# Splitting z and v in the opening of an attention and mixture-of-experts kernel

## Chip, cores and metric

The kernel runs on one core of a Trainium2 chip, as one program. The metric is the device time of one execution in microseconds. The core's engines are TensorE (PE; its weight loads are PEld), VectorE (DVE), ScalarE (ACT), GpSimd (POOL) and SyncE (SP), which issues most DMAs. Each works through its own queue in order.

## The reference

```python
def _attn_ref(u, v, z):                 # u, v: 8 x 3072 x 256, z: 8 x 3072 x 64
    scores = (1.0 / S) * np.matmul(z, z.transpose(0, 2, 1))
    attn = np.maximum(scores, 0.0) ** 2
    return (u * np.matmul(attn, v)).astype(np.float32)

def _moe_ref(x, w_gate, w1, w2, capacity):      # 8 experts, 1024 hidden, capacity 768
    expert_idx = np.argmax(x @ w_gate, axis=1)  # gate_w: its softmax probability
    # the first `capacity` tokens of each expert, in order, are kept
    h = np.maximum(np.einsum('ecd,edf->ecf', disp, w1), 0.0)
    y = np.einsum('ecf,efd->ecd', h, w2)
    # out[i] = gate_w[i] * y[expert, slot] for kept tokens, else 0
```

The inputs are float32, and so is the output of 24576 x 256.

## The kernel before

The experts fill up with the early tokens, so attention is computed only for the first 14 blocks of 512 queries (two batches and two blocks more), with a fallback for other data. Products run in float16 with each float32 operand split in two: a high half, and a low half that is the residue. Three matmuls (high by high, high by low, low by high) make one product.

For a block of queries the keys are taken in pairs of 128-row tiles. For each pair `team` (line 935) computes the scores: six matmuls of 64 rows and 512 columns (line 958), two at a time in the upper and lower 64 partitions. For that `zz` holds z transposed twice: in plane 0 the high half lies in partitions 0 to 63 and the low half above it, in plane 1 the two are swapped. `follow` (line 964) then makes the pair's weights: relu of each key tile and the square on ScalarE (lines 975 and 980), the high half as a cast on VectorE (`hi`, line 984) and the residue on VectorE (`lo`, line 993). The sums (line 1141) are matmuls of 128 x 256 with these weights and v's two halves: 24 for a pair, into four accumulators (`c`), two key tiles (`jj`) each. v's halves come from `v_piece`: high on ScalarE (line 524), low on VectorE (line 527).

z's groups of four tiles come from `z_group` (line 409): `hi` scales and rounds, `lo` (lines 421 and 422) copies the high half behind the place of the low half, so that three 64-wide parts stand in a row (high, low, high), and takes the residue. `tr` turns columns 0 to 127 and columns 64 to 191 of each tile on TensorE, four transposes for each plane (line 433), and `ev` copies each plane out of PSUM (line 437). Groups 3 to 5 go another way (`z_wide`, with DMA transposes).

All scaling is by powers of two from a maximum. v's scale needs all of the first batch's v: absolute sums and maxima of each piece (lines 493 and 75), a maximum over them (line 501), GpSimd's all-reduce (line 79), and two steps on the exponent bits (lines 60 and 62).

The order of the opening is written out by hand. `to_scores` and `to_sums` call `go(chain, n)`, which issues the next n steps of a chain; `A` are v's maxima, `G` z's groups, `V` v's pieces (tiles 0, 1, and 2 with 3), `follow[0]` and `follow[1]` the weights of pairs 0 and 1, `third` those of pair 2, `Z` the z groups that are turned by DMA. `warm_up(n)` issues n matmuls whose results are not used; they fill TensorE's time. After `to_sums`, a planner (`weave`, line 268) issues each chain's next step as soon as its modelled engine clocks (`clk`, with the costs written beside each step) let it fit. `steps` (line 1054) gives the order of the sums: in the first block all four accumulators of a pair, and in each accumulator both key tiles, one after the other.

Of the kernel before, what the change touches and what calls it, by code (L numbers as in the profile page):

```python
# [9 lines left out]
F32 = mybir.dt.float32  # L10
F16 = mybir.dt.float16
I32 = mybir.dt.int32
AF = mybir.ActivationFunctionType
ALU = mybir.AluOpType
# [4 lines left out]
P = 128  # L19
# [9 lines left out]
def attention_moe_kernel(ctx: ExitStack, tc: tile.TileContext, u, v, z, w_gate, w1, w2, out, cap):  # L29
# [311 lines left out]
    def prepare(bt, first=False, swap=(), held=None):  # L341
# [67 lines left out]
        def z_group(g):  # L409
            sl = slice(4 * g, 4 * g + 4)  # L410
            st = Bag()

            def hi():
                st.zhl = sb.tile([P, 4, 3 * DQ], F16, tag="zhl", name="zhl", bufs=3)
                if g < 2:
                    ts(st.zhl[:, :, 0:DQ], bt.zraw[:, sl], bt.zs, ALU.mult)
                else:
                    nc.scalar.activation(st.zhl[:, :, 0:DQ], bt.zraw[:, sl], AF.Copy, scale=bt.zs)

            def lo():  # L420
                nc.vector.tensor_copy(st.zhl[:, :, 2 * DQ:3 * DQ], st.zhl[:, :, 0:DQ])
                nc.vector.scalar_tensor_tensor(out=st.zhl[:, :, DQ:2 * DQ], in0=bt.zraw[:, sl], scalar=bt.zs,
                                               in1=st.zhl[:, :, 0:DQ], op0=ALU.mult, op1=ALU.subtract)

            def tr():
                if g < 2:
                    st.tp = [ps.tile([P, 4, P], F16, tag="sc", name="ztp", bufs=6) for r in range(2)]
                else:
                    t = ps.tile([P, 2, 4, P], F16, tag="sc", name="ztp", bufs=6)
                    st.tp = [t[:, r] for r in range(2)]  # L430
                for r in range(2):
                    for k in range(4):
                        nc.tensor.transpose(st.tp[r][:, k, :], st.zhl[:, k, r * DQ:r * DQ + P], ident)

            def ev(r):
                def f():
                    (nc.scalar.copy if r and g != 1 else nc.vector.tensor_copy)(
                        bt.zz[:, r, g * BLK:(g + 1) * BLK].rearrange("p (t q k) -> p t k q", t=2, k=2),
                        st.tp[r].rearrange("p (t k) q -> p t k q", k=2))
                return f  # L440

            return [[("ACT", 0.4, hi, None) if g > 1 else ("DVE", 0.3, hi, None)], [("DVE", 0.6, lo, key("zl", g))],
                    [("PE", 0.45, tr, None)],
                    [("DVE" if g == 1 else "ACT", 0.6 if g == 1 else 0.48, ev(1), key("ze", g)),
                     ("DVE", 0.6, ev(0), key("z", g))]]
# [74 lines left out]
        def v_piece(t0, k):  # L520
            o, i, a = slice(t0, t0 + k), t0 // 4, t0 % 4

            def hi():
                nc.scalar.activation(bt.v2[:, o, 0, :], bt.vraw[i][:, a:a + k], AF.Copy, scale=bt.vs)

            def lo():
                nc.vector.scalar_tensor_tensor(out=bt.v2[:, o, 1, :], in0=bt.vraw[i][:, a:a + k], scalar=bt.vs,  # L527
                                               in1=bt.v2[:, o, 0, :], op0=ALU.mult, op1=ALU.subtract)
                for j in range(t0 + 2, t0 + k, 2):
                    done[key("v", j // 2)] = clk["DVE"]  # L530

            return [[("ACT", 0.19 + 0.21 * k, hi, None)], [("DVE", 0.06 + 0.285 * k, lo, key("v", t0 // 2) if t0 + k > t0 // 2 * 2 + 1 else None)]]

        def factor():
# [68 lines left out]
        def go(c, n=1):  # L603
            for _ in range(n):
                assert c.item() is not None
                c.emit()
# [20 lines left out]

        def to_sums(follow, more):

            go(A[2])  # L630
            go(follow[0], 3)
            go(A[3])
            go(follow[0])
            go(A[4])
            warm_up(2)
            third = more()[0]
            go(G[2])
            go(A[6])
            go(A[5])
            go(follow[1], 2)  # L640
            vr = Chain([[("DVE", 0.2, v_red, None)], [("POOL", 0.4, v_all, None)], [("DVE", 0.6, v_bits, key("vs"))]], -2,
                       need_max("m", NM))
            go(vr, 3)
            go(follow[0])
            warm_up(11)
            go(G[2])
            warm_up(2)
            more()
            warm_up(3)
            Z = Chain(pipe([z_wide(t0) for t0 in range(NT, JT, ZW)]) + [[z_swap(0), z_swap(1)]], -2, late)  # L650
            for t, k in ((0, 1), (1, 1), (2, 2)):
                V[t] = Chain(v_piece(t, k), -2, done[key("vs")])
            go(V[0])
            go(V[1])
            go(V[0])
            go(V[1])
            go(follow[1])
            go(V[2])
            go(G[2])
            go(follow[1], 2)  # L660
            go(V[2])
            go(G[2])
            go(Z)
            go(third, 2)
            go(Z, 4)
            go(third)
            for i in range(2, JT // 2):
                Chain(v_piece(2 * i, 2), -2, done[key("vs")], gate=("pair", i - 2 + (2 < i < 6)))
# [194 lines left out]
    def attention(blocks, hook):  # L863
# [100 lines left out]
        def follow(p, s, w, t):  # L964
# [14 lines left out]
                sq[p] = sb.tile([P, 2, w], F32, tag="a", name="a")  # L979
                nc.scalar.activation(sq[p], sct.pop(p), AF.Square)  # L980

            def hi():
                hl = sb.tile([P, 2, nt, 2, HB], F16, tag="hl", name="hl", bufs=NHL)
                nc.vector.tensor_copy(hl[:, :, :, 0, :], sq[p].rearrange("p j (t k) -> p j t k", k=HB))  # L984
                prs[p] = lambda h, jj, c: hl[:, jj, c // 2, h, c % 2 * P:(c % 2 + 1) * P]
                if cornered(p):
                    own = prs[p]
                    prs[p] = lambda h, jj, c: corner[n][:, 2 * h + jj, c * P:(c + 1) * P] if c < 2 else own(h, jj, c - 2)
                sq[p] = (sq[p], hl)

            def lo():
                a, hl = sq[p]
                nc.vector.tensor_sub(hl[:, :, :, 1, :], a.rearrange("p j (t k) -> p j t k", k=HB), hl[:, :, :, 0, :])  # L993

            def turn(c):
                def f():
# [22 lines left out]
            def room_for():  # L1019
# [2 lines left out]
            st = [[("ACT", 0.05 + w * 0.00084, relu(0), None), ("ACT", 0.05 + w * 0.00084, relu(1), (aid, "r", k))],  # L1022
                  [("ACT", 0.09 + w * 0.00168, square, (aid, "s", k))],
                  [("DVE", 0.07 + w * 0.00107, hi, None, bt.key("vs"), room_for), ("DVE", 0.29 + w * 0.0021, lo, (aid, "a", p))]]
            if p + 1 < NP and cornered(p + 1):
                st.append([turn(0), turn(1)])
            if cc == CC and (ib, g // 2) in bt.kept:
# [26 lines left out]
        def steps():  # L1054

            for n, (_, _, _, cc) in enumerate(blocks):
                i = 0
                while i < NPAIR:
                    both = cc == CC and (i == 0 and not (opening and n == 0) or i == NPAIR - 2)
                    for h in range(2 if both else 1):  # L1060
                        for j in range(2 if both else 1):
                            for c in (2 * h, 2 * h + 1) if both else range(cc):
                                calm[0] = n * NPAIR + i < NP - 2 and both and (h + j > 0 if i else n > 0 and h + j < 2)
                                turning[0] = both and (i > 0 or n > 0 and h + j < 2)
                                yield n * NPAIR + i + j, c
                    i += 2 if both else 1

        def ld_u(n):
# [32 lines left out]
            scores_to(0)  # L1101
        clear[0] = open_bank
        operand = {}
        for p, c in steps():
            where[:] = p, c
            n, g = at(p)
            bt, ib, c0, cc = blocks[n]
            i = p % NPAIR
            if c == 0:
                hook(p)  # L1110
                done.setdefault(("pair", p), clk["PE"])
                loads_to(p + 4)
                if i == 0:
                    acc[n] = {}
                if i == NPAIR // 2:
                    ld_u(n)
            if c % (cc // 2) == 0:
                scores_to(p + 3 if p > 3 else p + 2 if p or c else 0)
                weave()
            if c == 0:  # L1120
                if is_next(p):
                    take(p)
                clk["PE"] = max(clk["PE"], need((aid, "a", p), bt.key("v", g),
                                                *([(aid, "d", n)] if cornered(p) else [])) + HOP)
                operand[p] = prs.pop(p)
            a = operand[p]
            if i == 0 and c % 2 == 0:

                k = bank[0] - 2
                if k in held:  # L1130
# [2 lines left out]
                bank[0] += 1  # L1133
                acc[n][c // 2] = ps.tile([P, 2, D], F32, tag="acc", name="acc", bufs=2)
            o = acc[n][c // 2][:, c % 2]
            for jj in (0, 1):
                j = 2 * g + jj


# [2 lines left out]
                                     stop=(i == NPAIR - 1 and jj + h == 2), skip_group_check=True)  # L1142
                op("PE", 0.328, 0.0)
                weave()
            if i == NPAIR - 1 and c % 2:
                drain(n, c // 2)
            if c == cc - 1:
                through.add(p)
                operand.pop(p)
            if i == NPAIR - 1 and c == cc - 1:  # L1150
# [359 lines left out]
```

## Time and profile before

| | |
|---|---|
| median of 3 runs | 777.61 us (776.28 to 780.22) |
| profiled execution, own time | 778.41 us |
| its span | 776.5 us |
| PE, DVE, ACT, POOL busy | 766.8, 514.4, 401.1, 116.6 us |
| granted TensorE clock | 0.998 of full speed |

The span is the time between the first and the last event of the trace; the execution's own time has a little around it. Busy time counts warm-up matmuls as well. In rows of the timeline, several like instructions in a row are merged (x2, x24), and what stands in brackets is the idle time of the engine before them and what ended it.

### The profile page before, as it was taken

The numbers are of one execution on the slowest core, as the hardware profiler recorded it, in microseconds if no ns is written. First come the engines' busy times: TensorE is split into PE (matmuls) and PEld (weight loads), VectorE is DVE, ScalarE is ACT, GpSimd is POOL, SyncE is SP. The second block draws the span as 40 slices with busy tenths as digits, with TensorE's granted clock in tenths as the row PEclk, the third lists the DMA queues.
The fourth block names the chain that finished last, engine by engine and source line by source line (L and its number), as shares of the span: only waits on it lengthen the run. The fifth ranks groups of instructions, "written<-read, shape, count | busy, mean of one in ns | idle before, by whom it ended". The sixth has DMA issues, their size and how long they took to land.

```text
span 776.5 us, 16291 instructions
## 1 busy us (share of the span) xinstructions
PE 766.8 (99%) x6474; PEld 572.3 (74%) x6474; DVE 514.4 (66%) x1134; ACT 401.1 (52%) x690; POOL 116.6 (15%) x122
## 2 busy tenths in 40 slices
PE   9999999999999999999999999999999999999996
PEld 3777878888887787878888877876666656666664
DVE  7998789754308799875554268889576575575741
ACT  6985558433016667573530057675455464463541
POOL 0000020210202020202022020203320321313302
PEclk9999999999999999999999999999999999999999
DMA  7699949999978979698789949882898955944001
GB/s 224 124 351 137 288 104 241 178 220 195 189 149 166 326 177 228 164 235 190 166 153 197 201 134 214 305 233 58 236 264 286 319 147 215 296 120 185 28 15 45
DMA packets 283831, 149.49 MB, mean 193 GB/s; under 512 B 229742, under 2 KB 255675, under 8 KB 283745
## 3 DMA queue, kind: packets, MB, share of 16 engines
q1 hardware_dynamic: 278848, 135.57, 71.8%
q0 software_dynamic: 4896, 12.79, 5.3%
q8 instruction: 52, 0.85, 0.4%
q14 instruction: 35, 0.28, 0.1%
HBM read 36.25 MB, written 59.92 MB: 124 GB/s over the span
## 4 chain that ended last, share of the span: by engine, by line
PE 88%; issue 3%; DMA 3%; DVE 2%; POOL 1%; SPq 1%; ACT 0%; POOLq 0%; ACTq 0%; DVEq 0%
PE acc L1141 51%; PE hps L1287 14%; PE yps L1311 14%; PE sc L958 8%; DMA ld<-kept 2%; DMA vraw<-in_v 1%; POOL out L86 1%; PE lg L722 1%; DVE hl L993 1%; SPq L375 0%; DVE hl L984 0%; DVE wm L75 0%; DVE xr L707 0%; DVE v L527 0%; SPq L369 0%
## 5 line engine op out<-in xcount | busy, mean ns | idle before, releaser
L1141 PE MATMUL acc<-v,hl 128*128 128x256 f16 x2280 | 260.7, 273 | 1.0 <-DVE v L527 0.6
L1141 PEld LDWEIGHTS <-hl 128*128 128x128 f16 x2280 | 219.5, 98 | 36.4 <-issue 9.2
L975 ACT ACTIVATE r<-sc 128x512 f32<-128x512 f32 (+1 forms) x212 | 105.5, 550 | 142.2 <-PE sc L958 140.0
L1311 PE MATMUL yps<-wt,hh 128*128 128x256 f16 (+1 forms) x776 | 126.8, 324 | 0.0
L1287 PE MATMUL hps<-fxt,wt 128*128 128x384 f16 (+2 forms) x816 | 126.7, 317 | 0.0
L993 DVE TENSOR_TENSOR hl<-a,hl 128x1024 f16<-128x1024 f32 (+1 forms) x106 | 118.1, 1114 | 3.5
L1287 PEld LDWEIGHTS <-wt 128*128 128x128 f16 x816 | 77.8, 98 | 47.1
L1311 PEld LDWEIGHTS <-hh 128*128 128x128 f16 x776 | 75.7, 98 | 48.4
L86 POOL DMA_INDIRECT disp<-xr,slot x54 | 56.8, 1051 | 359.7 <-issue 215.5
L1141 PE MATMUL acc<-v,ld 128*128 128x256 f16 x960 | 109.0, 273 | 0.6 <-DMA ld<-kept 0.6
L980 ACT ACTIVATE a<-r 128x1024 f32<-128x1024 f32 (+1 forms) x106 | 102.6, 968 | 5.0 <-DVE hl L993 2.6
L1141 PEld LDWEIGHTS <-ld 128*128 128x128 f16 x960 | 92.7, 98 | 13.9 <-issue 2.1
L984 DVE CAST hl<-a 128x1024 f16<-128x1024 f32 (+1 forms) x106 | 67.5, 637 | 45.8 <-ACT a L980 45.0
L1273 DVE SCALAR_TENSOR_TENSOR hh<-hps,hh 128x384 f16<-128x384 f32 (+2 forms) x136 | 70.6, 530 | 34.6 <-ACT hh L1272 33.1
L1272 ACT ACTIVATE hh<-hps 128x384 f16<-128x384 f32 (+2 forms) x136 | 63.4, 470 | 48.9 <-PE hps L1287 47.3
L86 POOL DMA_INDIRECT out<-ys,sid x48 | 53.3, 1111 | 129.9 <-DVE ys L1320 77.1
L958 PE MATMUL sc<-zz 64*128 64x512 f16 (+1 forms) x636 | 68.5, 355 | 0.0
L704 ACT ACTIVATE xr<-x,rsr 128x256 f16<-128x256 f32 x54 | 24.4, 500 | 82.9 <-DVE rsr L62 66.7
L1317 ACT ACTIVATE ys<-yps,sg 128x256 f32<-128x256 f32 x48 | 22.7, 474 | 76.9 <-PE yps L1311 70.4
L1320 DVE SCALAR_TENSOR_TENSOR ys<-yps,sg,ys 128x256 f32<-128x256 f32 x47 | 22.7, 483 | 53.0 <-ACT ys L1317 50.6
L1141 PE MATMUL acc<-v,nx 128*128 128x256 f16 x504 | 57.4, 273 | 0.0
L1141 PEld LDWEIGHTS <-nx 128*128 128x128 f16 x504 | 49.0, 98 | 6.5 <-issue 0.8
(135 smaller groups left out, 485.7 us busy)
## 6 DMA issues: line engine op xcount, KB each, us to landing
out<-zero SPq DMA_DIRECT2D x48, 512.0 KB
kept<-hl SPq DMA_DIRECT2D x40, 512.0 KB
wraw<-in_moe_w SPq DMA_DIRECT2D x32, 512.0 KB
vraw<-in_v SPq DMA_DIRECT2D x18, 512.0 KB
u<-in_u SPq DMA_DIRECT2D x13, 512.0 KB
zraw<-in_z SPq DMA_DIRECT2D x2, 768.0 KB
zz<-zz SPq DMA_DIRECT2D x4, 384.0 KB
xt<-xr SPq DMA_TRANSPOSE x54
```

The source lines that it names most:

```text
L86: r = nc.gpsimd.indirect_dma_start(out=dst, out_offset=bass.IndirectOffsetOnAxis(ap=idx, axis=0), in_=src, in_offset=None, bounds_check=bo ...
L704: return lambda: nc.scalar.activation(st.x16[:, c, 0:D], st.x[:, c, :], AF.Copy, scale=st.rs[:, c:c + 1])
L958: nc.tensor.matmul(s[jj][:, 0:w], lhsT=bt.zz[rows, (kl + jj) % 2, j * P:(j + 1) * P], rhs=bt.zz[rows, (ql + jj) % 2, q0:q0 + w], start=(i ...
L975: nc.scalar.activation(sct[p][:, jj, :], s[jj][:, 0:w], AF.Relu)
L980: nc.scalar.activation(sq[p], sct.pop(p), AF.Square)
L984: nc.vector.tensor_copy(hl[:, :, :, 0, :], sq[p].rearrange("p j (t k) -> p j t k", k=HB))
L993: nc.vector.tensor_sub(hl[:, :, :, 1, :], a.rearrange("p j (t k) -> p j t k", k=HB), hl[:, :, :, 0, :])
L1141: nc.tensor.matmul(o, lhsT=a(h, jj, c), rhs=bt.v2[:, j, l], start=(i + jj + h + l + c % 2 == 0), stop=(i == NPAIR - 1 and jj + h == 2), sk ...
L1272: Chain([[("ACT", 0.05 + w * 0.00083, lambda: nc.scalar.activation(th, src, AF.Relu), None)], [("DVE", 0.07 + w * 0.00104, lambda: nc.vect ...
L1273: [("DVE", 0.07 + w * 0.00104, lambda: nc.vector.scalar_tensor_tensor(out=tl, in0=src, scalar=0.0, in1=th, op0=ALU.max, op1=ALU.subtract), ...
L1287: nc.tensor.matmul(o, lhsT=wx.w1[:, d, wp, f * P:(f + 1) * P], rhs=sx.xt[:, xp * DC + d, a:a + w], start=(q == 0), stop=(q == len(seq) - 1))
L1311: nc.tensor.matmul(y[:, 0 if end else l], lhsT=hid(i, f)[:, sl], rhs=w[:, l], start=(f + i == 0 and l != 1), stop=(f == FC - 1 and i == 1) ...
```

## The change

`z_group` keeps only two parts (high, low). For plane 0 the tile is turned whole as before. For plane 1 the low and the high half are turned apart, each into its half of the partitions, so four transposes of 64 columns each way take the place of four of 128 columns, and `lo` no longer copies. The third group's `lo` runs on GpSimd as a product and a subtraction. In the opening, pair 0's residue and pair 1's square, high half and residue are made one key tile at a time, v's tiles 2 and 3 get their low halves one by one, and the sums of pairs 0 and 1 run over all four accumulators with the first key tile and then over all four with the second. The hand-written order is rearranged, and 16 warm-up matmuls stand where 18 stood in `to_sums`.

```diff
-                st.zhl = sb.tile([P, 4, 3 * DQ], F16, tag="zhl", name="zhl", bufs=3)
+                st.zhl = sb.tile([P, 4, 2 * DQ], F16, tag="zhl", name="zhl", bufs=3)
...
-                nc.vector.tensor_copy(st.zhl[:, :, 2 * DQ:3 * DQ], st.zhl[:, :, 0:DQ])
-                nc.vector.scalar_tensor_tensor(out=st.zhl[:, :, DQ:2 * DQ], in0=bt.zraw[:, sl], scalar=bt.zs,
-                                               in1=st.zhl[:, :, 0:DQ], op0=ALU.mult, op1=ALU.subtract)
+                if g < 2:
+                    nc.vector.scalar_tensor_tensor(out=st.zhl[:, :, DQ:], in0=bt.zraw[:, sl], scalar=bt.zs,
+                                                   in1=st.zhl[:, :, 0:DQ], op0=ALU.mult, op1=ALU.subtract)
+                else:
+                    t = sb.tile([P, 4, DQ], F32, tag="u", name="zsc", bufs=1)
+                    nc.gpsimd.tensor_scalar(out=t, in0=bt.zraw[:, sl], scalar1=bt.zs, scalar2=None, op0=ALU.mult)
+                    nc.gpsimd.tensor_tensor(out=st.zhl[:, :, DQ:], in0=t, in1=st.zhl[:, :, 0:DQ], op=ALU.subtract)
 
...
-                for r in range(2):
-                    for k in range(4):
-                        nc.tensor.transpose(st.tp[r][:, k, :], st.zhl[:, k, r * DQ:r * DQ + P], ident)
+                for k in range(4):
+                    nc.tensor.transpose(st.tp[0][:, k, :], st.zhl[:, k, :], ident)
+                for k in range(4):
+                    for r in (1, 0):
+                        nc.tensor.transpose(st.tp[1][DQ * (1 - r):DQ * (2 - r), k, :], st.zhl[:, k, DQ * r:DQ * (r + 1)],
+                                            ident)
...
-            return [[("ACT", 0.4, hi, None) if g > 1 else ("DVE", 0.3, hi, None)], [("DVE", 0.6, lo, key("zl", g))],
+            return [[("ACT", 0.4, hi, None) if g > 1 else ("DVE", 0.3, hi, None)], [("DVE", 0.6, lo, key("zl", g)) if g < 2 else ("POOL", 1.0, lo, key("zl", g))],
...
+            def lo_one(j):
+                def f():
+                    nc.vector.scalar_tensor_tensor(out=bt.v2[:, t0 + j, 1, :], in0=bt.vraw[i][:, a + j], scalar=bt.vs,
+                                                   in1=bt.v2[:, t0 + j, 0, :], op0=ALU.mult, op1=ALU.subtract)
+                return f
+
...
+            if first and t0 == 2:
+                return [[("ACT", 0.61, hi, None)], [("DVE", 0.38, lo_one(0), None), ("DVE", 0.38, lo_one(1), key("v", 1))]]
...
+            go(G[2])
             go(A[2])
             go(follow[0], 3)
             go(A[3])
...
             warm_up(2)
             third = more()[0]
+            warm_up(3)
             go(G[2])
+            go(follow[0])
+            go(follow[1])
             go(A[6])
             go(A[5])
-            go(follow[1], 2)
-            vr = Chain([[("DVE", 0.2, v_red, None)], [("POOL", 0.4, v_all, None)], [("DVE", 0.6, v_bits, key("vs"))]], -2,
+            vr = Chain([[("DVE", 0.2, v_red, None)], [("POOL", 0.4, v_all, None)], [("DVE", 0.4, v_bits, key("vs"))]], -2,
                        need_max("m", NM))
             go(vr, 3)
             go(follow[0])
-            warm_up(11)
-            go(G[2])
+            go(follow[1], 2)
+            warm_up(9)
+            more()
             warm_up(2)
-            more()
-            warm_up(3)
...
             go(V[1])
             go(follow[1])
             go(V[2])
-            go(G[2])
-            go(follow[1], 2)
+            go(follow[1], 3)
             go(V[2])
-            go(G[2])
+            go(follow[1])
+            go(V[2])
+            go(G[2], 2)
             go(Z)
...
-            def hi():
+            def hi_tile():
                 hl = sb.tile([P, 2, nt, 2, HB], F16, tag="hl", name="hl", bufs=NHL)
-                nc.vector.tensor_copy(hl[:, :, :, 0, :], sq[p].rearrange("p j (t k) -> p j t k", k=HB))
...
+            def hi():
+                hi_tile()
+                a, hl = sq[p]
+                nc.vector.tensor_copy(hl[:, :, :, 0, :], a.rearrange("p j (t k) -> p j t k", k=HB))
...
+            def square_half(j):
+                def f():
+                    if j == 0:
+                        sq[p] = sb.tile([P, 2, w], F32, tag="a", name="a")
+                    nc.scalar.activation(sq[p][:, j], sct[p][:, j], AF.Square)
+                return f
...
+            def hi_half(j):
+                def f():
+                    if j == 0:
+                        hi_tile()
+                    a, hl = sq[p]
+                    nc.vector.tensor_copy(hl[:, j, :, 0, :], a[:, j].rearrange("p (t k) -> p t k", k=HB))
+                return f
...
+            def lo_half(j):
+                def f():
+                    a, hl = sq[p]
+                    nc.vector.tensor_sub(hl[:, j, :, 1, :], a[:, j].rearrange("p (t k) -> p t k", k=HB), hl[:, j, :, 0, :])
...
+            if opening and p < 2:
+                if p == 1:
+                    st[1] = [("ACT", 0.53, square_half(0), None), ("ACT", 0.53, square_half(1), (aid, "s", k))]
+                    st[2] = [("DVE", 0.4, hi_half(0), None), ("DVE", 0.4, hi_half(1), None)]
+                else:
+                    st[2] = [("DVE", 0.65, hi, None)]
+                st[2] += [("DVE", 0.65, lo_half(0), None), ("DVE", 0.65, lo_half(1), (aid, "a", p))]
...
-                                yield n * NPAIR + i + j, c
+                                if not (opening and n == 0 and i < 2):
+                                    yield n * NPAIR + i + j, c, (0, 1)
+                    if opening and n == 0 and i < 2:
+                        for jj in (0, 1):
+                            for c in range(cc):
+                                yield i, c, (jj,)
...
-        for p, c in steps():
+        for p, c, jjs in steps():
...
-            if c == 0:
+            if c == 0 and jjs[0] == 0:
...
-            for jj in (0, 1):
+            for jj in jjs:
```

The further conditions on `jjs` keep hooks, scores and the end of a pair to its first or last round.

## Rows read from the trace of the kernel before

**Rows 1.** The page's first part: busy time, share of the span, instructions, by engine.
```profile
PE 766.8 (99%) x6474; PEld 572.3 (74%) x6474; DVE 514.4 (66%) x1134; ACT 401.1 (52%) x690; POOL 116.6 (15%) x122
```

**Rows 2.** Whom TensorE waited for: total us, times, longest.
```profile
PE acc L1141 <- DVE v L527: 0.6, 2, 0.5
PE acc L1141 <- DMA ld<-kept: 0.6, 2, 0.3
```

**Rows 3.** The chain of waits, whole span: start, length in us, what.
```profile
18.12 1.22 DVE hl L993
...
199.64 7.29 DMA ld<-kept
```

**Rows 4.** Timeline, 17 to 32 us: start, us, engine, line, operation, out<-in, count.
```profile
17.04 1.06 ACT L975 ACTIVATE r<-sc 128x512 f32<-128x512 f32 x2
...
18.05 0.15 DVE L62 TENSOR_SCALAR vsr<-vse 128x1 int32<-128x1 int32 x1
...
18.24 0.91 ACT L524 ACTIVATE v<-vraw,vsr 128x256 f16<-128x256 f32 x2
...
19.25 0.88 DVE L527 SCALAR_TENSOR_TENSOR v<-vraw,vsr,v 128x256 f16<-128x256 f32 x2
19.79 2.85 PE L1141 MATMUL acc<-v,hl 128*128 128x256 f16 x24 [0.45 <-DVE v L527]
...
20.85 1.23 DVE L993 TENSOR_TENSOR hl<-a,hl 128x1024 f16<-128x1024 f32 x1
...
22.00 0.75 DVE L527 SCALAR_TENSOR_TENSOR v<-vraw,vsr,v 128x512 f16<-128x512 f32 x1
...
22.66 0.73 DVE L437 COPY zz<-ztp 128x512 f16<-128x512 f16 x1
...
25.40 1.47 PE L958 MATMUL sc<-zz 64*128 64x512 f16 x12
25.59 1.22 DVE L993 TENSOR_TENSOR hl<-a,hl 128x1024 f16<-128x1024 f32 x1
...
26.80 5.41 PE L1141 MATMUL acc<-v,hl 128*128 128x256 f16 x48
...
28.11 1.23 DVE L993 TENSOR_TENSOR hl<-a,hl 128x1024 f16<-128x1024 f32 x1
```

**Rows 5.** Timeline, 9 to 17 us.
```profile
9.25 0.23 DVE L421 COPY zhl<-zhl 128x256 f16<-128x256 f16 x1
...
9.86 0.49 ACT L418 ACTIVATE zhl<-zraw,zb 128x256 f16<-128x256 f32 x1
...
10.71 2.15 DVE L437 COPY zz<-ztp 128x512 f16<-128x512 f16 x3
...
10.85 0.62 PE L433 MATMUL ztp<-ident,zhl 128*128 128x128 f16 x8 [0.30 <-DVE zhl L422]
...
14.19 2.55 PE L153 MATMUL warm<-ones 128*128 128x512 f16 x11
...
15.87 0.19 ACT L493 ACTIVATION_READ_ACCUMULATOR junk<-vraw 128x1 f32 x1
...
16.41 0.63 ACT L493 ACTIVATE junk<-vraw 128x512 f32<-128x512 f32 x1 [0.36 <-DMA vraw<-in_v]
```

**Rows 6.** Groups by form, 500 to 520 us: busy us, mean ns, idle before.
```profile
L993 DVE TENSOR_TENSOR hl<-a,hl 128x512 f16<-128x512 f32 x9 | 6.2, 691 | 0.3
...
L984 DVE CAST hl<-a 128x512 f16<-128x512 f32 x8 | 3.4, 421 | 0.0
```

**Rows 7.** Groups by form, 8 to 34 us: v's low half, one tile at a time.
```profile
L527 DVE SCALAR_TENSOR_TENSOR v<-vraw,vsr,v 128x256 f16<-128x256 f32 x2 | 0.9, 480 | 0.0
```

**Rows 8.** GpSimd in the timeline: its first all-reduce.
```profile
8.02 0.37 POOL L79 PARTITION_ALL_REDUCE nma<-nm  x1 [6.76 <-DVE nm L392]
```

**Rows 9.** GpSimd's costliest group on the page: busy us, mean ns, idle before.
```profile
L86 POOL DMA_INDIRECT out<-ys,sid x48 | 53.3, 1111 | 129.9 <-DVE ys L1320 77.1
```

**Rows 10.** SyncE's queue, 100 to 210 us: whom it waited for.
```profile
SPq L926 <- PE acc L1141: 8.4, 4, 3.3
```

More of the change, by code (lines that the diff above doesn't have):

```diff
@@ L993, in lo @@
                 nc.vector.tensor_sub(hl[:, :, :, 1, :], a.rearrange("p j (t k) -> p j t k", k=HB), hl[:, :, :, 0, :])
+            def square_half(j):
[15 more added lines that the diff above has]
+                    nc.vector.tensor_sub(hl[:, j, :, 1, :], a[:, j].rearrange("p (t k) -> p t k", k=HB), hl[:, j, :, 0, :])
+                return f
             def turn(c):
@@ L1116, in attention @@
                     ld_u(n)
-            if c % (cc // 2) == 0:
+            if c % (cc // 2) == 0 and jjs[0] == 0:
                 scores_to(p + 3 if p > 3 else p + 2 if p or c else 0)
                 weave()
-            if c == 0:
+            if c == 0 and jjs[0] == 0:
                 if is_next(p):
@@ L1126, in attention @@
             a = operand[p]
-            if i == 0 and c % 2 == 0:
+            if i == 0 and c % 2 == 0 and jjs[0] == 0:
                 k = bank[0] - 2
@@ L1144, in attention @@
                 weave()
-            if i == NPAIR - 1 and c % 2:
+            if i == NPAIR - 1 and c % 2 and jjs[-1] == 1:
                 drain(n, c // 2)
-            if c == cc - 1:
+            if c == cc - 1 and jjs[-1] == 1:
                 through.add(p)
```

## The prediction

> **What bounds the kernel now.** I read the page's busy line first: TensorE is busy for 766.8 of 776.5 us [rows 1]. Only idle or filler time ahead of its real work can be won. The waits of TensorE are short: 0.6 us for v's low half (line 527) and 0.6 us for the kept blocks [rows 2]. Both v waits lie in the opening, where warm-up matmuls fill the time until the first sums. So the question is what sets the start of the sums and whether they then run on. The chain of waits over the whole span passes, in the opening, through VectorE's residue step of pair 0 at 18.12 us [rows 3], and from 22.8 us on it is nearly all TensorE.
>
> The timeline then shows the opening engine by engine [rows 4]. v's scale is known at 18.20 us (18.05 + 0.15). VectorE is then busy with pair 0's residue (line 993) from 18.12 until v's low halves begin at 19.25; v's first high half had been ready since about 18.7 (18.24 and half of 0.91). TensorE resumes at 19.79. After 18.12 VectorE never rests: pair 1's residue at 20.85, v at 22.00, the copy of z's third group at 22.66, pair 2's residue at 25.59 to 26.81, pair 3's at 28.11 to 29.34. TensorE starts pair 2's sums at 26.80, and its third matmul (0.11 each: 5.41 us for 48) needs that residue at about 27.02. So in front of pair 2 TensorE has only 0.2 us to spare against VectorE, 0.15 after the 0.06 us between a VectorE end and TensorE's start (19.25 + 0.48 to 19.79). In front of pair 3 it has 0.36 us (26.80 + 24 x 0.112 + 0.22 = 29.70 against 29.34), less the same 0.06.
>
> **The change part by part.** I follow each engine in the order the new code issues.
>
> *z's groups 0 and 1.* Each loses a copy of 0.23 us on VectorE [rows 5], of which overlap leaves some 0.15, and gains four transposes: eight take 0.62, twelve at most 0.93. Half-width transposes are not in the trace; the bounds are 0 and 0.31 us per group, and I take 0.3, the same line's price. Group 0's set ended at 10.55 (0.30 idle before 10.85); it now starts 0.15 earlier and ends at 10.7, group 1's set starts there instead of at 10.85 and ends 0.15 later. VectorE's copies of group 1 (the last two of the three in 2.15 us) wait for them: 0.15 later, bounds -0.15 and +0.3. What follows on VectorE before 16.41 (two maxima, pair 0's high half, then one half residue of 0.69 [rows 6] where group 2's copy and residue stood, about 0.6) has 0.1 us of room, because the last v maximum waits for its DMA until 16.41. Value: 0 to 0.1 us late.
>
> *ScalarE ahead of the maximum.* Pair 1's first relu moves into the idle 0.36 us before 16.41. ScalarE is free at 16.06, the relu takes 0.53 (half of the 1.06 of rows 4), so the last absolute sum starts at 16.48 to 16.59. That and the line above delay v's scale by about 0.1 (bounds 0 and 0.3): known at 18.30. Pair 1's square in halves costs ScalarE no cover: half of it stands before the scale is known, and ScalarE reaches pair 2's square a few tenths earlier than before.
>
> *VectorE from the scale to pair 2's residue.* Pair 0's residue: one half remains, 0.69 [rows 6] where 18.12 to 19.25 is 1.13: -0.44, or -0.5 with the usual overlap. v's first low half so starts at 18.85 and ends at 19.33 (0.48 [rows 7]). Pair 1 in halves: 2 x 0.42 + 2 x 0.69 = 2.22 [rows 6] against 1.87 (20.13 to 22.00), a loss of 0.35, with 0.08 us of overlap at each of three joints only 0.1: I take +0.2. v's tiles 2 and 3 apart: 2 x 0.44 (half of 0.88 at 19.25) against 0.66 (22.00 to 22.66): +0.22. Sum with the late scale: 0.1 - 0.47 + 0.2 + 0.22 = +0.05, which is nothing; best -0.2 (0 - 0.5 + 0.1 + 0.2), worst +0.43 (0.3 - 0.44 + 0.35 + 0.22). So pair 2's residue ends where it ended, near 26.8.
>
> *TensorE.* It resumes at 19.4 (19.33 + 0.06), 0.4 earlier. The new order (all four accumulators with tile 0, then with tile 1) has the same 24 matmuls per pair and needs v's second tile and the second half 1.34 us later, so neither pair stalls: VectorE has v's tile 2 ready at about 21.5 (19.77 for v's tile 1, two high halves, one residue half, 0.44) and tile 3 at 22.6, and TensorE asks for them at 22.0 and 23.4. The scores of pairs 4 and 5 then start at about 24.65 instead of 25.40, 0.75 earlier, pair 2's sums at 26.05, and their third matmul waits for the residue until 26.87. In terms of an unbroken run pair 2 starts at 26.65 where it started at 26.80. Gain: 0.15 from the spare time, plus what VectorE gains or loses; with ScalarE's lead I take 0.2. Of the 0.75 us won, 0.55 is given back there.
>
> *Group 2's residue on GpSimd.* It leaves VectorE (counted above) and its two instructions run from 10.35 (9.86 + 0.49 [rows 5]). GpSimd arithmetic on this shape is not in the trace. Nearest rows: its all-reduce, 0.37 [rows 8], and its indirect DMA, 1.11 [rows 9]: 0.7 to 2.2 for the two; I take 1.0, nearer to the reduction, which is also arithmetic on GpSimd. The end, 11.1 to 12.6, lies well before TensorE comes to group 2's transposes (about 15.0: behind pair 2's scores, which ended before the 14.19 of the warm-ups, and three warm-ups). Cost 0. The all-reduce of v's maximum, behind the last absolute sum, finds GpSimd free.
>
> *Later.* From pair 4 on TensorE waits for no residue today [rows 2]. Its later waits (kept blocks) start from a load that SyncE's queue issued after TensorE had freed the buffer [rows 10]; the chain at 199.64 has that load's 7.29 us [rows 3]. They move along with TensorE, so a shift survives.
>
> Sum: the profiled execution's own time is 778.41 us (span 776.5 and 1.9 around it); less 0.2 gives 778.2. The median of the runs is 0.80 below it (777.61), so the forecast is **777.4 us**.
>
> **The rivals.**
> *VectorE comes out at its best bound.* Overlap between the halves is full, the half-width transposes cost nothing. Pair 2's residue ends 0.2 earlier and the gain is 0.35 to 0.5, with pair 3's spare 0.3 and VectorE's own 0.2 as the ceiling: 777.0. For it: ScalarE has room, overlaps are seen at each joint. Against it: four more VectorE instructions.
> *The gain is lost later.* The order after the opening is planned from modelled clocks that change a little, and one new wait of the size of rows 2 (0.3 us) eats it: 777.6. For it: spare times of 0.2 to 0.4 in the opening; against it: TensorE waits nearly nowhere else.
> *Slower: VectorE is the bound and gets more work.* Place: pair 2's residue. At the worst bound it ends 0.43 later, at 27.24, and TensorE's third matmul goes from 27.02 to 27.30: +0.28, or 777.9. A GpSimd that holds VectorE up at 10.35 to 12.6 adds to it: group 1's residue (0.48) and the copies run there; if all of 0.5 us came through to the scale, +0.7 in all: 778.3. It decides once that residue ends after 26.96. The Trainium skill (GPSIMD Engine Reference, "Key points") says that GpSimd shares its SBUF interfaces with VectorE and contends with instructions that have two SBUF inputs or run in a 2-port mode. By it group 1's residue would be touched and the copies out of PSUM would not; no run here shows it.
> *Slower: GpSimd is not ready for this arithmetic.* TensorE takes its queue in order, so late group 2 transposes hold back nine warm-ups (2.55/11 each, 2.1 us), pair 3's scores and the sums. It decides from an end of GpSimd's pair at about 15.0, and costs one for one from there. Rows 8 show 6.76 us of GpSimd idle before its first reduction, in which a preparation could hide; a second one of that length would put the pair's end at 8.39 + 6.76 + 2.2 = 17.35: +2.3, or 779.9; a third before v's all-reduce, +6.5: 784. The Trainium skill (GPSIMD Engine Reference, "Instruction dispatch") has the first call into freshly loaded code at about 6 us. Against it: what ends GpSimd's idle time ahead of its 48 indirect DMAs is mostly data from VectorE [rows 9], not a preparation of its own.
>
> **How the numbers follow.** Forecast (gain 0.05 to 0.35): 0.50. Best bound: 0.15. Lost later: 0.15. More VectorE work: 0.12. GpSimd not ready: 0.08, half of it beyond 3.9 us. All but the last lie within 0.7 us, less than the three runs scatter (776.28 to 780.22), so the range is that scatter about the forecast, 775.5 to 779.5, wide enough for each case but the last. About 0.5% (3.9 us) is what a measurement tells from no change: slower by that 0.04, faster 0.03 for what I have not seen, within 0.93.
>
> **What would show it.** TensorE's first long run of sums begins near 19.4; scores of pairs 4 and 5 near 24.65; then a new wait of about 0.5 us for VectorE inside pair 2's first matmuls; pair 2's residue ends at 26.6 to 26.9. GpSimd's two instructions end before 12.6. If the residue ends before 26.4 the first rival holds; if group 2's transposes start after 15.3, the last. A change of over 1 us with the opening as forecast would make the argument on later waits wrong.

## The result and the profile after

The changed kernel takes 785.86 us (median of 6 runs, 784.46 to 786.48) against 777.74: ratio 1.0101, 95% interval 1.0084 to 1.0119. It is 8.1 us slower; the forecast was 777.4 with a range up to 779.5. The profiled execution has a span of 784.6 us and a time of 786.42.

The page's first part, to set beside [rows 1]: TensorE is busy for 769.2 us, 2.4 more, and its share has fallen. The rest of the loss, 5.7 of 8.1 us in the span, is idle time.

```profile
PE 769.2 (98%) x6484; PEld 572.8 (73%) x6484; DVE 513.9 (65%) x1134; ACT 401.5 (51%) x691; POOL 119.1 (15%) x124
```

TensorE's waits (whom it waited for, us in total, times, longest) name a new one, which no row of [rows 2] has.

```profile
PE ztp L436 <- POOL zhl L427: 4.2, 1, 4.2
PE acc L1196 <- DVE hl L1015: 1.1, 2, 0.8
```

The timeline of GpSimd alone (start, us, line, operation, tiles; in brackets the idle time before it) shows the cause. In the kernel before, GpSimd's only work between its first memsets and 48 us was two all-reduces, at 8.02 [rows 8] and 17.47.

```profile
7.97 0.37 POOL L79 PARTITION_ALL_REDUCE nma<-nm  x1 [6.71 <-DVE nm L392]
17.29 0.93 POOL L426 TENSOR_SCALAR zsc<-zraw,zb 128x256 f32<-128x256 f32 x1 [8.95 <-ACT junk L500]
18.30 0.68 POOL L427 TENSOR_TENSOR zhl<-zsc,zhl 128x256 f16<-128x256 f32 x1
25.16 0.38 POOL L79 PARTITION_ALL_REDUCE vma<-vmx  x1 [6.19 <-issue]
```

The product's inputs (z and its scale) were there at 8.9 us and the high half that the subtraction also reads at 10.3, yet the product starts at 17.29, and the all-reduce of v's maximum, whose input was there at 17.3, starts at 25.16. The name behind the 8.95 us is a guess of the view: ScalarE's absolute sums have nothing to do with the product. The fourth line's idle time carries no releaser but "issue". Nothing in the profile accounts for either gap but GpSimd itself. The queues that the page calls "instruction" carry the same in the profiles before and after (52 packets on one, 35 and 34 on the other), so no extra transfer of code shows there.

The timeline of all engines shows what hung on it. It answers to [rows 4] and [rows 5].

```profile
14.00 0.82 PE L153 MATMUL warm<-ones 128*128 128x512 f16 x3
...
19.03 0.61 PE L436 MATMUL ztp<-ident,zhl 128*128 128x128 f16 x4 [4.21 <-POOL zhl L427]
...
20.14 4.02 PE L153 MATMUL warm<-ones 128*128 128x512 f16 x9
...
25.77 0.15 DVE L62 TENSOR_SCALAR vsr<-vse 128x1 int32<-128x1 int32 x1
...
27.03 5.29 PE L1196 MATMUL acc<-v,hl 128*128 128x256 f16 x47 [0.25 <-DVE v L540]
...
32.15 0.75 DVE L540 SCALAR_TENSOR_TENSOR v<-vraw,vsr,v 128x512 f16<-128x512 f32 x1 [0.43 <-ACT v L531]
...
32.25 1.47 PE L976 MATMUL sc<-zz 64*128 64x512 f16 x12
...
33.54 1.23 DVE L1015 TENSOR_TENSOR hl<-a,hl 128x1024 f16<-128x1024 f32 x1
...
34.82 1.38 PE L1196 MATMUL acc<-v,hl 128*128 128x256 f16 x11 [0.77 <-DVE hl L1015]
```

TensorE ran out of filler at 14.8 and stood for 4.2 us at the third group's transposes. v's scale is known at 25.92 instead of 18.20 (25.77 + 0.15, against [rows 4]), the first long run of sums starts at 27.03 instead of 19.79. In front of pair 2 VectorE holds it up for another 0.77 us. Pair 4's sums, at 34.19 in the kernel before, start at

```profile
42.04 4.16 PE L1196 MATMUL acc<-v,hl 128*128 128x256 f16 x36
```

which is 7.85 us later; from there the two traces run about alike (the first matmuls of the experts, 519.49 before and 527.15 after, are 7.7 apart). So nearly the whole loss lies in the first 42 us.

A table by stretch (us, busy time of each engine, granted clock, DMA share, GB/s) shows a side effect. After the 4.2 us without matmuls the granted clock is at 0.50, the 1.2 GHz level, through the third group's transposes and the nine warm-ups. It rises during pair 3's scores and is at 1.00 from 25.30, before the sums. Neither the slow clock nor the 4.2 us adds to the loss here, since all this work is over at 25.3 to 25.9 and TensorE then still waits 0.65 us for pair 0's residue, which VectorE makes behind v's scale (first sum at 26.51).

```profile
14.80:19.03 4.23, 0.02 (x1) 0.00 (x1) 2.22 (x5) 3.33 (x8) 1.61 (x2) 0.89 0.38 68
19.03:24.10 5.07, 5.07 (x23) 1.94 (x23) 0.00 (x0) 0.00 (x0) 0.00 (x0) 0.50 0.02 3
24.10:27.03 2.93, 2.03 (x10) 0.58 (x10) 1.42 (x5) 1.08 (x3) 0.38 (x1) 0.85 0.00 0
```

### The profile page after: what moved, and what is told of

It reads as the page before. It is cut to its first block, busy times and chain, and to the rows that moved or that the text cites. A ratio compares the mean times of both kernels' runs of the same rounds, so it can differ in the third digit from the quotient of the medians.

```text
span 784.6 us, 16320 instructions
## 1 busy us (share of the span) xinstructions
PE 769.2 (98%) x6484; PEld 572.8 (73%) x6484; DVE 513.9 (65%) x1134; ACT 401.5 (51%) x691; POOL 119.1 (15%) x124
## 4 chain that ended last, share of the span: by engine, by line
PE 87%; issue 4%; DMA 3%; DVE 2%; ACT 2%; POOL 1%; SPq 0%; POOLq 0%; ACTq 0%
PE acc L1196 50%; PE hps L1342 14%; PE yps L1366 14%; PE sc L976 7%; DMA ld<-kept 2%; DMA vraw<-in_v 1%; POOL out L86 1%; PE lg L740 1%; DVE hl L1015 1%; ACT a L998 0%; ACT r L993 0%; ACT junk L500 0%; DVE hl L1011 0%; DVE wm L75 0%; ACT v L531 0%
## 5 line engine op out<-in xcount | busy, mean ns | idle before, releaser
L1015 DVE TENSOR_TENSOR hl<-a,hl 128x1024 f16<-128x1024 f32 (+1 forms) x104 | 115.7, 1112 | 3.5
```

## The experiments

The theory after the result, called "code" in the expectations: GpSimd's all-reduce and its arithmetic (product, subtraction) are two kinds of work whose code is not there at the same time, and each change of kind costs a load. That the gap is a load of code is a reading, since no row names it; in the run with one addition below no DMA packet at all is recorded from 17.7 to 23.5 us, inside one of the gaps. Shown below are the gap, its sizes and the kinds that bring it. The rivals: the rest of the change costs the time ("rest"), or the arithmetic itself is slow or held up ("slow arithmetic").

**GpSimd taken out.** One part of the changed kernel undone (the planner's entry for this step goes back to VectorE with it; the code is shortened):

```diff
-                if g < 2:
-                    nc.vector.scalar_tensor_tensor(...)
-                else:
-                    nc.gpsimd.tensor_scalar(...); nc.gpsimd.tensor_tensor(...)
+                nc.vector.scalar_tensor_tensor(out=st.zhl[:, :, DQ:], ...)      # all groups
```

> The changed kernel with one part undone: the third group's residue is again one VectorE instruction, at the place in the order where GpSimd's two stood; all else as changed. Theory 'code' (two kinds of work on GpSimd, the all-reduce and the arithmetic, each need their code brought in, and that costs the 9.0 and 6.2 us of idle GpSimd in the trace after): all of the loss goes, v's scale is known near 18.5, and the time is 777.3 to 778.3, because VectorE has 0.4 us more ahead of v's last maximum. Rival 'rest' (the split into tiles, the half-width transposes or the new order of the sums cost the time): it stays above 781. Rival 'slow arithmetic' (GpSimd's two instructions are late because VectorE or ScalarE hold it up): also 777.3 to 778.3, so this run doesn't part it from 'code'.

Measured: 777.93 us, ratio 1.0005 (0.9991 to 1.0019). All of the loss is gone, so "rest" falls. Its timeline is close to the forecast's, with a longer wait in front of pair 2:

```profile
17.10 0.16 DVE L503 TENSOR_REDUCE vmx<-vm 128x1 f32<-128x8 f32 x1
...
19.21 5.29 PE L1191 MATMUL acc<-v,hl 128*128 128x256 f16 x47 [0.25 <-DVE v L535]
...
24.32 0.75 DVE L535 SCALAR_TENSOR_TENSOR v<-vraw,vsr,v 128x512 f16<-128x512 f32 x1 [0.44 <-ACT v L526]
...
24.43 1.47 PE L971 MATMUL sc<-zz 64*128 64x512 f16 x12
...
25.71 1.23 DVE L1010 TENSOR_TENSOR hl<-a,hl 128x1024 f16<-128x1024 f32 x1
...
26.99 4.26 PE L1191 MATMUL acc<-v,hl 128*128 128x256 f16 x37 [0.77 <-DVE hl L1010]
```

```profile
34.22 5.46 PE L1191 MATMUL acc<-v,hl 128*128 128x256 f16 x48
```

**One column of arithmetic.** The kernel before with a GpSimd addition that nothing waits for (the line that makes its tile is left out):

```diff
             allmax(bt.nma, bt.nm, 1)
+            nc.gpsimd.tensor_tensor(out=tiny, in0=zero[:, 0:1], in1=zero[:, 1:2], op=ALU.add)
```

> The kernel before with one GpSimd addition of 128x1 more, behind the all-reduce of z's maximum; nothing reads its result. 'Code': the all-reduce of v's maximum, at 17.47 before, comes at 20 to 25, the sums start 3 to 7.5 us late, and the time is 781 to 785. 'Slow arithmetic' or 'rest': an addition of one column is over in 0.2 us and nobody waits for it, so the all-reduce stays at 17.5 and the time at 777.7.

Measured: 785.24 us (two runs), ratio 1.0095 (1.0069 to 1.0122), just above the 781 to 785 expected. GpSimd's timeline:

```profile
7.88 0.37 POOL L79 PARTITION_ALL_REDUCE nma<-nm  x1 [6.61 <-DVE nm L392]
17.49 0.18 POOL L399 TENSOR_TENSOR tiny<-zero 128x1 f32<-128x1 f32 x1 [9.24 <-issue]
23.54 0.38 POOL L79 PARTITION_ALL_REDUCE vma<-vmx  x1 [5.86 <-issue]
```

The addition takes 0.18 us and has no input to wait for; still it starts 9.24 us after the all-reduce, and the next all-reduce 5.86 us after it. "Slow arithmetic" falls: 0.18 us of unread work costs 7.7 us, nearly as much as the whole change. In the trace v's all-reduce comes 6.1 us later than before and pair 4's sums 7.1 (41.27 against 34.19); the next run shows what the difference is.

**The part alone.** The kernel before with the residue of the third group on GpSimd and nothing else (the lines of the change, without the removal of the copy).

> The kernel before with only one part of the change: the third group's residue on GpSimd as a product and a subtraction; the copy of the high half stays on VectorE. 'Code': the product starts near 17.3, the transposes of group 3 near 19, v's all-reduce near 25.2, the sums near 26.5: 784 to 785. 'Slow arithmetic': the two instructions take longer but v's all-reduce is not held up beyond them: 778 to 780. 'Rest': 777.7.

Measured: 788.45 us (two runs), ratio 1.0137 (1.0112 to 1.0161), more than the 784 to 785 expected. GpSimd's rows are about where they were foreseen:

```profile
17.68 0.93 POOL L427 TENSOR_SCALAR zsc<-zraw,zb 128x256 f32<-128x256 f32 x1 [9.23 <-ACT r L980]
18.70 0.67 POOL L428 TENSOR_TENSOR zhl<-zsc,zhl 128x256 f16<-128x256 f32 x1
25.41 0.38 POOL L79 PARTITION_ALL_REDUCE vma<-vmx  x1 [6.04 <-issue]
```

Most of the surplus lies in the first sums. v's all-reduce is 7.94 us later than before, pair 4's sums are 9.54 later (43.73). In between, TensorE stands without filler until 26.75 and then runs its sums at the slow clock:

```profile
26.75 0.37 PE L1146 MATMUL acc<-v,hl 128*128 128x256 f16 x1 [4.77 <-ACT v L529]
27.75 7.26 PE L1146 MATMUL acc<-v,hl 128*128 128x256 f16 x47 [0.62 <-DVE v L532]
```

The granted clock is 0.50 from 26.75 to 31.5 and 1.00 from 32.0; the same 47 matmuls take 5.29 us at 1.00 in the changed kernel. The run before this one has it too: 5.90 us without matmuls, then 6.67 us for 47 sums, at 0.50 until 28.0. The changed kernel, which has its warm-ups behind the late transposes, starts its sums at 1.00 and doesn't pay this. What is left of the surplus, 0.9 us, comes after pair 4; this profile has 2.1 us of waits for kept blocks where [rows 2] has 0.6.

**The same addition elsewhere.** First behind the all-reduce of v's maximum (`allmax(bt.vma, ...)`):

> The kernel before with the same unread GpSimd addition of 128x1, now behind the all-reduce of v's maximum; GpSimd's next all-reduce is wanted about 30 us later. 'Code': two loads again, but both lie in GpSimd's idle time: 777.7, within 0.5. The addition starts about 6 us after the all-reduce if the 9.2 us of the first load came from the DMA traffic of that stretch, about 9 us if that code is simply longer to bring in. Rival 'mixing' (a program with both kinds pays something everywhere): above 779.

Measured: 777.72 us, ratio 1.0002 (0.9987 to 1.0018). The gap before the addition is there, 6.93 us, in time when nobody wants GpSimd. A second one in front of the next all-reduce can't be seen: if there is one, it lies in the 27.21 us for which GpSimd waits for VectorE there. "Mixing" falls.

```profile
17.06 0.36 POOL L79 PARTITION_ALL_REDUCE vma<-vmx  x1 [8.78 <-DVE vmx L501]
24.35 0.31 POOL L508 TENSOR_TENSOR tiny<-zero 128x1 f32<-128x1 f32 x1 [6.93 <-issue]
51.87 0.38 POOL L79 PARTITION_ALL_REDUCE wgma<-wgm  x1 [27.21 <-DVE wgm L75]
```

The 6.93 us lie between the 6 and the 9 that the expectation told apart, so it doesn't decide what makes the first gap longer.

Then ahead of the first all-reduce, behind GpSimd's memset:

> The kernel before with the same unread addition ahead of the first all-reduce, right behind GpSimd's memset. 'Code': if the arithmetic is at hand when the program starts, it runs at once, and the load for the all-reduce starts a little later than the 1.3 us of before; since it has until 8.0, the time is 777.7 or at most 1 us more. If the arithmetic had to be loaded at the start too, z's maximum waits 6 us or more: 784 or above.

Measured: 787.50 us, ratio 1.0129 (1.0108 to 1.0150). The second case holds. The arithmetic does not start at once at the program's start either: the addition waits 7.77 us behind the memset, and z's all-reduce comes at 17.65 instead of 8.02.

```profile
9.04 0.18 POOL L124 TENSOR_TENSOR tiny<-zero 128x1 f32<-128x1 f32 x1 [7.77 <-issue]
17.65 0.38 POOL L79 PARTITION_ALL_REDUCE nma<-nm  x1 [8.43 <-issue]
```

These two runs bear on a rival that the theory did not name: that GpSimd only waits for the DMA traffic of the opening to end. Four gaps that begin between 8.3 and 9.2 us, the three before arithmetic behind z's all-reduce and the one before the all-reduce here, end between 17.29 and 17.68, just after that traffic has died down (its share is 0.28 to 0.41 from 16.0 to 16.5 us and at most 0.16 from 16.5 to 17.0). But the addition here starts at 9.04, in the middle of the traffic (share 0.96 from 4 to 9 us), and the 6.93 us of the late addition as well as the 5.86 to 6.19 us before v's all-reduce lie where there is next to none. So the traffic alone doesn't make the gap, though it may lengthen it.

**Which kinds bring the gap.** A memset, and a cast of the third group's size, in the place of the addition:

> The kernel before with a GpSimd memset of 128x1 behind the all-reduce of z's maximum, where the earlier run had an addition; nothing reads it. 'Code': GpSimd's memset ran before anything was loaded (at 0.26 us), so it should belong to no loaded code and cost nothing: all-reduce of v's maximum near 17.4, 777.7. If any other instruction between two all-reduces costs a load: 781 to 786.

> The same place, now a GpSimd copy of 128x256 from float32 to float16 that nothing reads: the size of the third group. It tells whether elementwise work as such needs the load, or only some kinds. 'Code' leaves both open: with a load 781 to 786, as the addition; without one 777.7, and its row gives the price of such a pass on GpSimd (the product took 0.93 us).

Measured: 778.11 us, ratio 1.0007 (0.9991 to 1.0024), and 777.92 us, ratio 0.9999 (0.9979 to 1.0020). GpSimd in the first and in the second:

```profile
7.93 0.16 POOL L399 MEMSET tiny<- 128x1 f32 x1
16.84 0.36 POOL L79 PARTITION_ALL_REDUCE vma<-vmx  x1 [8.75 <-DVE vmx L504]
```

```profile
8.60 0.45 POOL L399 CAST tiny<-zero 128x256 f16<-128x256 f32 x1
17.51 0.36 POOL L79 PARTITION_ALL_REDUCE vma<-vmx  x1 [8.45 <-DVE vmx L504]
```

Neither waits after the all-reduce, and the next all-reduce comes on time. So not every elementwise pass brings the gap: memset and cast don't, the product and the addition do. The subtraction ran only behind a product, so it was not tested alone.

**Is there a gain in the rest?** The residue of the third group on VectorE, issued between the two steps where VectorE waits for the all-reduce (`go(vr)`, `go(G[2])`, `go(vr, 2)`), with pair 3's scores ahead of the transposes:

> As the first, but the third group's residue on VectorE stands where VectorE waits for GpSimd's all-reduce of v's maximum (0.5 us idle there in both traces), the scores of pair 3 come ahead of the third group's transposes, and the warm-up matmuls are laid out to suit (19 in all). 'Code': v's scale near 18.3, sums from about 19.4, then the wait in front of pair 2 that the prediction names; 777.0 to 777.6, faster than before by 0.2 to 0.7 at the most. 'Rest': above 781. If the residue delays the scale, the sums start after 19.8 and the time is 778 or more.

Measured: 777.33 us, ratio 0.9990 (0.9974 to 1.0005): within the expectation, and not to be told from no change. The wait in front of pair 2 is 0.73 us. Then with `go(third, 2)` for `go(third)` at the end of `to_sums`, which swaps two VectorE instructions and nothing else:

> As the run with the residue in the gap, with one swap on VectorE alone: pair 2's high half is issued by hand ahead of the low half of v's tiles 4 and 5, as the kernel before had it (the planner put it behind, where VectorE idles 0.44 us for ScalarE). Theory 'planned order' (the 0.73 us wait in front of pair 2 is longer than the forecast 0.55 because of that swap): VectorE's idle 0.44 goes, the wait falls to about 0.3, and the time to 776.9 to 777.3. Rival 'amount of work' (VectorE simply has too much to do with the halves): the wait stays at 0.6 to 0.7 and the time at 777.3 or above.

Measured: 777.95 us, ratio 1.0005 (0.9993 to 1.0017), above what "planned order" expected. The wait in front of pair 2 is gone, but VectorE's idle time moved on, to v's next piece, and TensorE now waits 0.53 us in front of pair 3. The timeline of VectorE in this run, and then TensorE's row:

```profile
24.58 0.74 DVE L535 SCALAR_TENSOR_TENSOR v<-vraw,vsr,v 128x512 f16<-128x512 f32 x1
25.24 1.22 DVE L1011 TENSOR_TENSOR hl<-a,hl 128x1024 f16<-128x1024 f32 x1
27.17 0.75 DVE L535 SCALAR_TENSOR_TENSOR v<-vraw,vsr,v 128x512 f16<-128x512 f32 x1 [0.71 <-ACT v L526]
```

```profile
29.84 2.58 PE L1192 MATMUL acc<-v,hl 128*128 128x256 f16 x22 [0.53 <-DVE hl L1011]
```

Then pair 1 and v's tiles 2 and 3 whole again:

> The last one with less split: pair 1's square, high half and residue and v's tiles 2 and 3 are made whole again, only pair 0's residue stays in halves. 'Amount of work': VectorE saves the 0.2 + 0.22 us that the prediction counted, pair 2's residue ends 0.4 earlier and the wait in front of it goes, against a new one of 0.2 to 0.3 in front of pair 1 (v's low half ends at about 22.3); in all 0.0 to 0.3 faster than the last, 776.7 to 777.2. If the split into tiles is what carries the gain, it is 0.3 or more slower than the last.

Measured: 777.90 us, ratio 1.0006 (0.9997 to 1.0015), where 776.7 to 777.2 was expected. TensorE does not wait in front of pair 2; it waits in front of pair 1 (0.43) and, new, for the DMA that swaps z's halves (0.63), so the work saved on VectorE moved nothing forward:

```profile
22.40 2.67 PE L1184 MATMUL acc<-v,hl 128*128 128x256 f16 x23 [0.43 <-DVE v L535]
...
32.98 1.68 PE L968 MATMUL sc<-zz 64*128 64x512 f16 x14 [0.63 <-DMA zz<-zz]
```

Last, as the run with the one swap (pair 1 and v's tiles 2 and 3 in halves), but with pair 1's high halves as GpSimd casts (`nc.gpsimd.tensor_copy` for `nc.vector.tensor_copy` in `hi_half`):

> The run with the order by hand, with pair 1's two high halves (casts of 128x512) on GpSimd as copies, the kind that the last run showed to need no load. 'Code': GpSimd does each in about 0.9 us (0.45 for half the size), v's all-reduce stays at 17.6, and nothing is held up. VectorE loses 0.75 us of work, pair 2's residue ends near 25.8 and the wait in front of pair 2 goes. If VectorE alone limits the opening, the sums of pair 4 start 0.3 to 0.6 earlier than in the runs so far and the time is 777.0 to 777.4; if ScalarE or the DMA copies that swap z's halves come next, as the last runs suggest, pair 4 starts where it did and the time is 777.5 to 778.0. If GpSimd beside VectorE slows VectorE's residues (0.68 for a half), pair 2's residue ends later than 26.5.

Measured: 777.53 us, ratio 0.9986 (0.9975 to 0.9997). The interval just excludes 1, but the kernel before ran at 778.68 in that comparison and at 777.5 to 777.7 in the others, and the opening of this trace is no earlier (pair 4's sums 17.54 us after v's last maximum, 16.98 before). I don't count it as a gain. Casts and VectorE's residues beside them:

```profile
18.18 0.61 POOL L1025 CAST hl<-a 128x512 f16<-128x512 f32 x1 [0.22 <-ACT a L1017]
...
18.25 1.07 DVE L1031 TENSOR_TENSOR hl<-a,hl 128x512 f16<-128x512 f32 x1
...
19.86 0.73 POOL L1025 CAST hl<-a 128x512 f16<-128x512 f32 x1 [1.08 <-ACT a L1017]
20.04 1.09 DVE L1031 TENSOR_TENSOR hl<-a,hl 128x512 f16<-128x512 f32 x1
...
21.45 0.68 DVE L1031 TENSOR_TENSOR hl<-a,hl 128x512 f16<-128x512 f32 x1
```

The two residues that run beside a cast take 1.07 and 1.09 us, the one that runs alone 0.68; pair 2's residue ends at 26.61, later than the 26.5 that the expectation set as the sign of this. The wait for the DMA swap is back:

```profile
33.12 1.69 PE L972 MATMUL sc<-zz 64*128 64x512 f16 x14 [0.72 <-DMA zz<-zz]
```

## Why the prediction was wrong

The step that failed is "Group 2's residue on GpSimd", with its "Cost 0" and "the all-reduce of v's maximum ... finds GpSimd free". I priced the two instructions by their run time: 1.0 taken, 0.7 to 2.2 as bounds, 0.93 + 0.68 = 1.61 measured, so the bounds held. What I left out of the sum stands between them and their neighbours: 8.95 us before the product and 6.19 us before the next all-reduce. The kernel before has 6.76 us of idle GpSimd ahead of its first all-reduce [rows 8], put down to VectorE; a preparation could hide under it. For the addition put there one of 7.77 us shows; for the all-reduce no run shows whether there is one.

The mechanism was among the rivals ("GpSimd is not ready for this arithmetic"), with its place and, worked out from that row, an end of the pair at 17.35 (measured 18.98), a loss of 6.5 us at v's all-reduce (7.8 measured, 25.16 against 17.35 in the run with GpSimd taken out) and 784 us. The sign that I named for it came true as well: the third group's transposes start at 19.03, after 15.3. I gave it 0.08, and the range ended at 779.5. The argument against it was weak: the 48 indirect DMAs of [rows 9] say nothing of a kind of instruction that no row showed. Nor are they GpSimd's costliest group, as [rows 9] calls them; the page of before has another above it, whose idle time is mostly put down to "issue", the word that stands at the 6.19 us gap too (what those waits were stays open):

```profile
L86 POOL DMA_INDIRECT disp<-xr,slot x54 | 56.8, 1051 | 359.7 <-issue 215.5
```

The Trainium skill (GPSIMD Engine Reference, "Instruction dispatch") gives about 6 us for the first call into freshly loaded code; the 5.86 to 6.19 us before the second all-reduce agree in size, the 9 us before the arithmetic don't, and here the gap is there again at the change back.

The other steps are read from the run with GpSimd taken out, counted from the start of v's last maximum (17.10 there; 17.21 before, so that a DMA that lands earlier doesn't count):

| step | predicted | measured |
|---|---|---|
| sums start earlier by | 0.4 | 0.47 (2.11 against 2.58) |
| scores of pairs 4 and 5 earlier by | 0.75 | 0.86 (7.33 against 8.19) |
| pair 2's residue ends later by | 0.05 (-0.2 to 0.43) | 0.24 (9.84 against 9.60) |
| new wait in front of pair 2 | 0.5 | 0.77 |
| pair 4's sums earlier by | 0.2 | -0.14 (17.12 against 16.98) |

Half-width transposes: twelve take 0.74 (9.74 to 10.48, both from the trace after) where eight took 0.62; I had taken 0.3 more and bounded it by 0 and 0.31. The idea that VectorE takes back what TensorE wins was right, and VectorE takes a little more: the planner puts v's next low half ahead of pair 2's high half, and VectorE waits 0.44 us for ScalarE there (24.32 in that timeline). That is the reshuffling of the later order that a rival named, at the place of the forecast's wait. The distance of 16.98 us is 16.98 to 16.99 in the runs with the late addition, the memset and the cast too, which have the old opening; 17.12 to 17.94 in the five that have the new one without GpSimd arithmetic, and 24.88 in the changed kernel. None of the new orders reaches pair 4 sooner.

What stays open: whether a different order of VectorE, ScalarE and the DMA swap together would gain the 0.4 us; the runs here removed a wait and met the next. A gain of that size would be hard to see in a whole run: from pair 4's sums to the experts' first matmul the four traces with the old opening and sums on time (the kernel before, the late addition, the memset, the cast) already differ by 2.9 us, 484.32 to 487.21. Why the gaps have the sizes they have is open too.

## What to carry to other kernels

Before work moves to an engine, ask of the trace whether that engine has done that kind of work in this program, next to its present kinds; a duration prices the instruction and not the change of kind. On GpSimd here a change between all-reduce and arithmetic (a product or an addition) costs 6 to 9 us each way, so it belongs where nobody wants GpSimd for that long; memset and casts brought no such gap. And where three engines run close behind each other, a piece saved on one is worth only the spare time of the next: look up that spare time first.

## What the runs showed of the hardware

- The gap before GpSimd's arithmetic was 8.95 to 9.24 us behind z's all-reduce, beside busy DMA queues (share 0.99 over 8.3 to 17.3 us), 7.77 at the program's start (share 0.86) and 6.93 in the quiet time after 17.4. The gap before the all-reduce was 8.43 us beside the traffic and 5.86 to 6.19 in the quiet time. So the gaps that lay in 8.3 to 17.7 us were 2.0 to 2.6 us longer; that the traffic is the reason was not tested by itself.
- A GpSimd product of 128x256 float32 took 0.93 us, a subtraction 0.68, a cast 0.45 (the product being the first instruction after the change of kind).
- After 5.90 and 4.77 us without matmuls TensorE's granted clock was 0.50 when the sums began, and the first 47 took 6.67 and 7.26 us instead of 5.29.
- VectorE residues with two inputs in SBUF took 1.07 to 1.09 us beside a GpSimd cast, and 0.68 alone: the contention that the Trainium skill (GPSIMD Engine Reference, "Key points") states, with its size here.
